# Order of the down units, of the ReLU sums and of a small key copy in a kernel of windowed attention and a low-rank mixer

## Chip, cores and metric

One core of a Trainium2 chip. The metric is the device time of one execution in microseconds (us). The engines have their own in-order queues and meet through semaphores: TensorE (PE, with its weight loads PEld), VectorE (DVE), ScalarE (ACT), GpSimd (POOL) and SyncE (SP, which issues most DMAs here).

## What is computed

Batch 4, 8 heads, 768 positions, head size 64; then a mixer over positions of rank 32 and a two-layer feed-forward of width 2048.

```python
scores = q @ k.T / sqrt(64) - slope[h] * dist      # dist: distance, or 96 for a global key outside the window
keep   = (pos_k < 8) | (0 <= pos_q - pos_k < 96)   # 8 global keys and a window of 96
a      = softmax(where(keep, scores, -1e9));  x = a @ v      # heads side by side: x is 768 x 512 per batch
u      = x + (x.T @ U @ V).T                       # U: 768 x 32, V: 32 x 768
out    = u + relu(u @ w_ch1) @ w_ch2               # 512 -> 2048 -> 512
```

## The kernel before

Attention goes pair of heads by pair of heads: 16 pairs, four to a batch. The pairs 0 to 3 are done in a first stage; from pair 4 on, a loop (L819) takes one step per pair, with i from 4 to 17 ("pair i" below is step i). In it stand the scores of pair i (L366, L373; 128-wide blocks of the diagonal and of the block before it), their scaling and distance term on DVE (L412, L406), the exponentials on ACT (L430), the product with the values of pair i-1 (L443, L447, then reciprocal L452 and scaling L466 on DVE, and a cast to fp16 on POOL, L469), and the mixer of pair i-1: M1 (L478), MT (L495, its result copied from PSUM by DVE at L496, the tile `tmp`), M3 (L532, added into x_sb by DVE at L537 and cast by POOL at L540). Keys and queries of pairs 8 to 15 are loaded in fp32, cast by ACT (L129), turned by DMA transposes that SP issues (L327, L330), and the keys of the neighbour block are put together in `kA` with the eight global keys in front: the rest by ACT (L339), the global columns by DVE (L340).

Between these steps stand slots: `fill(n)` (L731) lets out n units of the feed-forward of an earlier batch. A unit is an "up" (L646: eight 128x256 matmuls into `hps`, then a ReLU on ACT into `htr`, L651) or a "down". Rows are taken in groups of 256, (b, g) with g from 0 to 2. `unit()` (L741) picks: a down may go when the ups of its group are all out and `held[0]` is false; otherwise an up, as long as the ups are not too far ahead; with both possible they alternate.

For batch 0 a down is four 128x512 matmuls (L681): tile t of 128 rows takes four of them (parts 0 to 3, one quarter of w_ch2 each) into one PSUM bank `cps`, opened by the mixer product L675, and DVE adds the bank into x_sb (L686). w_ch2 comes in four pieces, issued by POOL at L230, one for each part.

For the other nine groups (`WG`) the second layer is a Strassen-like product of seven instead of eight (L690, the units x1 y1 x2 y2 x3 y3 x4 on the banks `cx` and `cy`). It needs sums of the ReLU output, s1 = a21 + a22, s2 = s1 - a11, s4 = a12 - s2, s3 = a11 - a21 (in the place of a21), and differences of w_ch2, t1 to t4. `queue_sums` (L621) is called after the fourth and the eighth up of a group and queues each sum in two halves as a job; after a unit, `fill` lets jobs out whose count has been passed (two a unit when more than four are queued, otherwise one). A job is one DVE instruction (L570). `need` (L574) lets out what a product needs and has not got yet. x2 needs s2, y2 s1, x3 s3, y3 s4.

The order of every engine's queue is the order of the program. PSUM has two banks `cps`, three banks `th` (for `hps`, and for the last part of the scores from pair 7 on), one pair `sc` (scores, and M3's result) and one `ob` (values, M1, MT).

Of the kernel before, what the change touches and what calls it, by code (L numbers as in the profile page):

```python
# [16 lines left out]
ALU = mybir.AluOpType  # L17
# [3 lines left out]
def kernel(  # L21
# [13 lines left out]
    nc = tc.nc  # L35
# [3 lines left out]
    P = 128  # L39
# [4 lines left out]
    NJC = DFF // P  # L44
    R = moe_U.shape[1]
    NP = H // 2
# [19 lines left out]
    HJ = NJC // 2  # L66
# [20 lines left out]
    def ps_cps(name):  # L87
        return psum.tile([P, 512], FP32, name=name, tag="cps", bufs=2)
# [29 lines left out]
    def cast_qk(i, *engs):  # L118
        got = []
        for st, nm, eng in zip(staged.pop(i), ("q16", "k16"), engs * 2):  # L120
            st16 = stp.tile([P, NSB, 2, D], FP16, name=nm, tag=nm, bufs=2)
            turn_over = eng.copy if eng is nc.scalar else eng.tensor_copy
            turn_over(st16.rearrange("p n h d -> p h n d"), st)
            got.append(st16)
        cast[i] = got
# [210 lines left out]
    def st_K(i):  # L336
        kT = kts[i]
        kA = kp.tile([P, NSB - 1, P], FP16, name="kA", tag="kA")
        nc.scalar.copy(kA[:, :, NG:], kT.rearrange("d (n p) -> d n p", n=NSB)[:, 0:NSB - 1, NG:])  # L339
        nc.vector.tensor_copy(  # L340
            kA[:, :, 0:NG], kT[:, 0:NG].unsqueeze(1).broadcast_to((P, NSB - 1, NG))
        )
        kas[i] = kA
# [223 lines left out]
    def queue_sum(name, part, out_, a, b_, op, wait=0):  # L567

        def go():
            nc.vector.tensor_tensor(out_, a, b_, op)  # L570
            have.add((name, part))
        (slow if name[0] == "t" else jobs).append((count[0] + wait, go))

    def need(*names):  # L574

        for queue, kind in ((jobs, tuple), (slow, str)):
            while not all(n in have for n in names if isinstance(n[0], kind)):
                queue.popleft()[1]()
# [32 lines left out]
    def queue_group(b, g):  # L611
        ts = slice(g * FT, (g + 1) * FT)
        uT, tmp16, x_sb = uTs[b], tmps[b], xs[b]
        n0, n1 = 2 * g, 2 * g + 1
        cell = {}

        split = (b, g) in WG
        follow = (b, g + 1) if g + 1 < NFG else (b + 1, 0)
        last = (b, g) == (B - 1, NFG - 1)

        def queue_sums(k):  # L621

            h = cell["htr"]
            if k == 0:
                for x in (1, 2, 4):
                    cell[f"s{x}"] = ffp.tile([P, HJ, P], FP16, name=f"s{x}", tag=f"s{x}", bufs=1)
                cell.update(a11=h[:, 0:HJ, 0:P], a12=h[:, HJ:NJC, 0:P],
                            a21=h[:, 0:HJ, P:FT], s3=h[:, 0:HJ, P:FT], a22=h[:, HJ:NJC, P:FT])
            js = slice(k * HJ // 2, (k + 1) * HJ // 2)
            for name, a, b_, op in (  # L630
                ("s1", "a21", "a22", ALU.add), ("s2", "s1", "a11", ALU.subtract),
                ("s4", "a12", "s2", ALU.subtract), ("s3", "a11", "a21", ALU.subtract),
            ):
                queue_sum((name, b, g), k, cell[name][:, js], cell[a][:, js], cell[b_][:, js], op, wait=0 if last else 2)

        def mk_up(at):
            jp = at // 2 + (at % 2) * NJC // 4 if split else at

            def go():
                if jp == 0:  # L640
                    cell["htr"] = ffp.tile([P, NJC, FT], FP16, name="htr", tag="htr", bufs=3)
                hps, done = begun.pop(jp) if jp in begun else (ps_th("hps"), 0)
                for k in range(2):
                    jt = 2 * jp + k
                    for dc in range(done, NDC):
                        nc.tensor.matmul(  # L646
                            hps[:, k * FT:(k + 1) * FT],
                            w1_16[:, dc, jt * P:(jt + 1) * P], uT[:, dc, ts],
                            start=(dc == 0 and k == 0), stop=(dc == NDC - 1 and k == 1),
                        )  # L650
                nc.scalar.activation(  # L651
                    cell["htr"][:, 2 * jp:2 * jp + 2].rearrange("p j t -> p (j t)"), hps, AF.Relu
                )
                if split and at % 4 == 3:
                    queue_sums(at // 4)
            return go

        def store(n, cs=slice(0, DM)):
            def go():
                nc.sync.dma_start(out[b, n * P:(n + 1) * P, cs], x_sb[:, n, cs])  # L660
            if b:
                go()
            else:
                kept.append(go)

        def mk_down(t, part):
            n = 2 * g + t

            def go():
                if (b, g, t, part) == (0, 0, 1, 0):  # L670
                    queue_weight_sums()
                if part == 0:
                    cell["cps"] = ps_cps("cps")
                    if b == 0:
                        nc.tensor.matmul(  # L675
                            cell["cps"], v16w[:, n * P:(n + 1) * P], tmp16,
                            start=True, stop=False,
                        )
                cps, htr = cell["cps"], cell["htr"]
                for jc in range(4 * part, 4 * part + 4):  # L680
                    nc.tensor.matmul(  # L681
                        cps, htr[:, jc, t * P:(t + 1) * P], w2_16[:, jc],
                        start=(b > 0 and jc == 0), stop=(jc == NJC - 1),
                    )
                if part == NJC // 4 - 1:
                    nc.vector.tensor_tensor(x_sb[:, n], cps, x_sb[:, n], ALU.add)  # L686
                    store(n)
            return go

        def mk_product(bank, half, a, w, dst, first=False, done=None):  # L690

            def go():
                if bank not in cell:
                    cell[bank] = ps_cps(bank)
                need(*(((a, b, g), k) for k in range(2) if a[0] == "s"))
                need(*((w, k) for k in range(4 if w == "t3" else 2) if w[0] == "t"))
                ps = cell[bank][:, half]
                for j in range(HJ):
                    nc.tensor.matmul(  # L699
                        ps, cell[a][:, j], weight(w, j), start=(first and j == 0),  # L700
                        stop=(done is not None and j == HJ - 1), skip_group_check=True,
                    )
                n, cs = dst
                nc.vector.tensor_tensor(x_sb[:, n, cs], ps, x_sb[:, n, cs], ALU.add)  # L704
                for what in done or ():
                    store(*what)
            return go

        if b:
            for at in range(NJC // 2):  # L710
                ups_q.append((mk_up(at), (b, g)))
        else:
            first_ups.append([(mk_up(at), (b, g)) for at in range(NJC // 2)])
        if split:
            x1 = mk_product("cx", lo, "a11", "b11", (n0, lo), first=True)
            x2 = mk_product("cx", lo, "s2", "t2", (n0, hi_))
            x3 = mk_product("cx", lo, "s3", "t3", (n1, hi_), done=[(n1, hi_)] if last else None)
            x4 = mk_product("cx", lo, "a22", "t4", (n1, lo), done=[(n1, lo)] if last else [(n1,)])
            y1 = mk_product("cy", lo, "a12", "b21", (n0, lo), first=True)
            y2 = mk_product("cy", hi_, "s1", "t1", (n1, hi_))  # L720
            y3 = mk_product("cy", hi_, "s4", "b22", (n0, hi_), done=[(n0,)])
            for made in (x1, y1, x2, y2, x3, y3, x4):
                downs_q.append((made, (b, g)))
        else:
            for t in range(2):
                for part in range(NJC // 4):
                    downs_q.append((mk_down(t, part), (b, g)))

    ahead, held, kept = [0], [True], deque()

    def fill(n):  # L731
        for _ in range(n):
            unit()
            count[0] += 1
            for _ in range(2 if len(jobs) > 4 else 1):
                for queue in (jobs, slow):
                    if queue and queue[0][0] < count[0]:
                        queue.popleft()[1]()
                        break
# [79 lines left out]
    for i in range(NP, NPAIR + 2):  # L819
# [69 lines left out]
        if live:  # L889
            st_E(i, 0)  # L890
            if i < NPE:
                st_P(i)
        fill(next(units))
        if i >= NPE:
            for _ in range(min(2, len(kept))):
                kept.popleft()()
# [14 lines left out]
            st_X(i - 1)  # L911
        if NPE <= i + 2 < NPE + 2:
            cast_qk(i + 2, nc.gpsimd)
        fill(next(units))
    while ups_q or downs_q:
        fill(1)
# [36 lines left out]
```

## Time and profile before

| what | value |
|---|---|
| three runs | 233.32, 231.82, 234.01 us; median 233.32 |
| profiled execution | 231.37 us; span from first to last instruction 229.6 us |
| granted TensorE clock | 0.998 |
| whole sum of L570 for t, 128x1024 | 0.68 us undisturbed |
| half sum of L570, 128x512 | 0.42 us undisturbed |
| scores' scaling L412 128x1024; L406 128x384 | 1.22 us; 0.55 us |
| eviction L686; adds L704; L537; tmp copy L496 | 0.69; 0.42; 0.96; 0.29 us |
| landing of the w_ch2 pieces after their issue | 7.4 to 14.5 us |

In the profile's rows a group of instructions has its line, engine, operation, tiles (out <- in), shape and count, then busy time in us and the mean of one in ns, then the idle time of the engine in front of them and what ended most of it. In a timeline a row has start, length, engine, line, operation and, in brackets, the idle time before it and its releaser. Matmuls of one run overlap: each starts 0.109 us after the one before at 256 columns (0.216 at 512), while it lasts 0.27 (0.38) to its modelled end.

### The profile page before, as it was taken

To read this page: it belongs to the slowest core of one execution; us is meant where nothing else is said; L and a number is where in the kernel's file an instruction comes from. 1 tells how busy PE (TensorE), PEld (TensorE's weight loads), DVE (VectorE), ACT (ScalarE), POOL (GpSimd) and SP (SyncE) were. 2 spreads that over 40 slices of the span, in tenths; PEclk is the share of its full clock that TensorE was granted. 3 is DMA by queue.
4 is the path that set the end of the run, shared out by engine and by line. 5 is a ranking of instruction groups with operands and counts; after the bars stand their busy time and mean duration, and the time that the engine had idled before them with its cause. 6 is when DMAs were issued, how large, how long until landed. Compare 5 with 4: busy or idle time off the path is not lost.

```text
span 229.6 us, 5883 instructions
## 1 busy us (share of the span) xinstructions
PE 219.3 (96%) x2418; PEld 172.0 (75%) x2420; DVE 158.6 (69%) x346; ACT 125.9 (55%) x196; POOL 70.7 (31%) x115
## 2 busy tenths in 40 slices
PE   7889999999989999998999989999999999999993
PEld 2446678788644546886888868888989888888882
DVE  3688775749586979597979887979764444444452
ACT  6677857685705253958485847392732433333320
POOL 6398637297543423131313131313111000000000
PEclk9999999999999999999999999999999999999999
DMA  6999999989998979999999993751321202010022
GB/s 203 280 291 237 267 221 246 303 159 179 193 170 188 201 184 238 219 232 217 215 245 174 261 178 97 129 174 30 92 67 34 94 0 94 0 69 26 8 86 93
DMA packets 86563, 36.68 MB, mean 160 GB/s; under 512 B 74152, under 2 KB 83592, under 8 KB 86536
## 3 DMA queue, kind: packets, MB, share of 16 engines
q1 hardware_dynamic: 81480, 32.01, 57.5%
q0 software_dynamic: 5056, 4.29, 12.5%
q8 instruction: 19, 0.31, 0.6%
q14 instruction: 8, 0.07, 0.1%
HBM read 27.46 MB, written 6.29 MB: 147 GB/s over the span
## 4 chain that ended last, share of the span: by engine, by line
PE 67%; DVE 11%; DMA 10%; ACT 5%; POOL 4%; issue 1%; SPq 1%; ACTq 0%
PE hps L646 25%; PE cx L699 13%; PE cy L699 10%; PE cps L681 8%; DMA w<-in_moe_w_ch_dram 6%; DMA vst<-in_v_dram 3%; DVE sp L412 3%; PE sc L366 2%; ACT ep L430 2%; PE ob L447 2%; DVE x_sb L466 1%; PE sc L532 1%; PE tp L254 1%; PE ob L443 1%; DVE x_sb L704 1%
## 5 line engine op out<-in xcount | busy, mean ns | idle before, releaser
L646 PE MATMUL hps<-uT,w 128*128 128x256 f16 x756 | 95.5, 273 | 0.2 <-ACT htr L651 0.2
L651 ACT ACTIVATE htr<-hps 128x512 f16<-128x512 f32 x96 | 56.4, 599 | 60.8 <-PE hps L646 60.6
L646 PEld LDWEIGHTS <-w 128*128 128x128 f16 x756 | 71.0, 98 | 9.6 <-issue 0.3
L412 DVE SCALAR_TENSOR_TENSOR sp<-sc,relcat 128x1024 f32<-128x1024 f32 (+1 forms) x27 | 32.1, 1189 | 8.0 <-ACT ep L430 4.3
L430 ACT ACTIVATE ep<-sp 128x1408 f16<-128x1408 f32 x24 | 33.2, 1383 | 0.0
L699 PEld LDWEIGHTS <-htr 128*128 128x128 f16 x288 | 27.7, 98 | 3.4
L704 DVE TENSOR_TENSOR x_sb<-cx,x_sb 128x256 f32<-128x256 f32 x36 | 15.2, 422 | 19.3 <-PE cx L699 18.6
L469 POOL CAST x<-x_sb 128x384 f16<-128x384 f32 x27 | 14.1, 522 | 46.6 <-DVE x_sb L466 43.6
L681 PE MATMUL cps<-w,htr 128*128 128x512 f16 x96 | 23.6, 379 | 1.1 <-DMA w<-in_moe_w_ch_dram 1.1
L540 POOL CAST x<-x_sb 128x768 f16<-128x768 f32 x12 | 11.0, 914 | 43.2 <-DVE x_sb L537 43.2
L699 PEld LDWEIGHTS <-s 128*128 128x128 f16 x216 | 20.2, 98 | 4.3 <-DVE s L570 2.0
L704 DVE TENSOR_TENSOR x_sb<-cy,x_sb 128x256 f32<-128x256 f32 x27 | 11.4, 422 | 12.5 <-PE cy L699 12.3
L466 DVE TENSOR_TENSOR x_sb<-ob,rcp 128x384 f32<-128x384 f32 x30 | 16.7, 558 | 1.0
L366 PEld LDWEIGHTS <-kT 64*128 64x128 f16 x192 | 8.5, 93 | 11.4 <-issue 10.1
L447 PE MATMUL ob<-v,ep 128*128 128x65 f16 x192 | 16.6, 193 | 0.0
L366 PE MATMUL sc<-qT,kT 64*128 64x128 f16 x192 | 15.7, 220 | 0.3 <-DVE x_sb L537 0.2
L681 PEld LDWEIGHTS <-htr 128*128 128x128 f16 x96 | 8.6, 97 | 9.4 <-issue 1.2
L447 PEld LDWEIGHTS <-ep 128*128 128x128 f16 x192 | 13.9, 98 | 2.3 <-issue 0.5
L443 PE MATMUL ob<-vA,ep 128*128 128x65 f16 x160 | 14.4, 194 | 0.4 <-DVE vA L316 0.2
L537 DVE TENSOR_TENSOR x_sb<-sc,x_sb 128x768 f32<-128x768 f32 x12 | 11.5, 956 | 4.6 <-PE sc L532 4.6
L142 POOL CAST v<-vst 128x768 f16<-128x768 f32 x16 | 13.4, 838 | 3.8 <-DMA vst<-in_v_dram 3.8
L373 PE MATMUL sc<-qT,kA 64*128 64x128 f16 x160 | 13.2, 216 | 0.3
(110 smaller groups left out, 320.1 us busy)
## 6 DMA issues: line engine op xcount, KB each, us to landing
qst<-in_q_dram SPq DMA_DIRECT2D x16, 384.0 KB, 5.4
kst<-in_k_dram SPq DMA_DIRECT2D x16, 384.0 KB, 6.4
vst<-in_v_dram SPq DMA_DIRECT2D x16, 384.0 KB, 4.1
out_dram<-x_sb SPq DMA_DIRECT2D x23, 256.0 KB, 3.3
w<-in_moe_w_ch_dram POOLq DMA_DIRECT2D x8, 512.0 KB, 8.6
vA<-v SPq DMA_DIRECT2D x8, 152.3 KB, 4.1
out_dram<-x_sb SPq DMA_DIRECT2D x2, 128.0 KB
uT<-x SPq DMA_TRANSPOSE x12, 3.1
```

Source lines behind the costliest of these rows:

```text
L366: nc.tensor.matmul(scs[hi][:, o:o + P], kT[r, kb * P:(kb + 1) * P], qT[r, kb * P:(kb + 1) * P], start=(o == 0 and not on_pe), stop=(o + P ...
L412: nc.vector.scalar_tensor_tensor(out=sps[i][:, :, c0:c0 + tot], in0=both[:, :, 0:tot], scalar=qk_scale / slope[2 * (i % NP)], in1=relfs[c0 ...
L430: nc.scalar.activation(eps[i][:, hi], sps[i][:, hi], AF.Exp, scale=slope[2 * (i % NP)])
L443: nc.tensor.matmul(ob[:, qi], ep[:, OF[qi - 1]:OF[qi - 1] + P], vA[:, qi - 1, hi], start=True, stop=False,)
L447: nc.tensor.matmul(ob[:, qi], ep[:, DG[qi]:DG[qi] + P], vt[:, qi, hi], start=(qi == 0), stop=True,)
L466: nc.vector.tensor_tensor(xo, ob[:, :, 0:D], rb, ALU.mult)
L469: nc.gpsimd.tensor_copy(x16, xo)
L646: nc.tensor.matmul(hps[:, k * FT:(k + 1) * FT], w1_16[:, dc, jt * P:(jt + 1) * P], uT[:, dc, ts], start=(dc == 0 and k == 0), stop=(dc == ...
L651: nc.scalar.activation(cell["htr"][:, 2 * jp:2 * jp + 2].rearrange("p j t -> p (j t)"), hps, AF.Relu)
L681: nc.tensor.matmul(cps, htr[:, jc, t * P:(t + 1) * P], w2_16[:, jc], start=(b > 0 and jc == 0), stop=(jc == NJC - 1),)
L699: nc.tensor.matmul(ps, cell[a][:, j], weight(w, j), start=(first and j == 0), stop=(done is not None and j == HJ - 1), skip_group_check=True,)
L704: nc.vector.tensor_tensor(x_sb[:, n, cs], ps, x_sb[:, n, cs], ALU.add)
```

## The change

Five edits. Batch 0's first group does the parts 0, 1 and 2 of both its tiles before part 3 of either; since both tiles are open at once, each has its own bank in `cell[t]`. `held[0]` is set anew ahead of the last slot of a step, so that the downs may begin in the last slot of pair 6 and not only in pair 7. In the groups of `WG` except the last, s3 and s4 are queued whole, once all eight ups are out, and s3 ahead of s4; the entries of the second call wait for one unit in place of two. The slot after the first exponential lets no jobs out (`quiet`), and the next unit lets one more out. The global key columns are copied by GpSimd.

In the order of the engines' queues, every unit from the last slot of pair 6 on stands one place sooner than before; DVE has 16 sums and 8 key copies fewer, and POOL the 8 copies, between the cast of v (L142) and the cast after M3 (L540).

```diff
         kA = kp.tile([P, NSB - 1, P], FP16, name="kA", tag="kA")
         nc.scalar.copy(kA[:, :, NG:], kT.rearrange("d (n p) -> d n p", n=NSB)[:, 0:NSB - 1, NG:])
-        nc.vector.tensor_copy(
+        nc.gpsimd.tensor_copy(
             kA[:, :, 0:NG], kT[:, 0:NG].unsqueeze(1).broadcast_to((P, NSB - 1, NG))
         )
...
-            js = slice(k * HJ // 2, (k + 1) * HJ // 2)
             for name, a, b_, op in (
                 ("s1", "a21", "a22", ALU.add), ("s2", "s1", "a11", ALU.subtract),
-                ("s4", "a12", "s2", ALU.subtract), ("s3", "a11", "a21", ALU.subtract),
+                ("s3", "a11", "a21", ALU.subtract), ("s4", "a12", "s2", ALU.subtract),
             ):
-                queue_sum((name, b, g), k, cell[name][:, js], cell[a][:, js], cell[b_][:, js], op, wait=0 if last else 2)
+                parts = {k: slice(k * HJ // 2, (k + 1) * HJ // 2)}
+                if name in ("s3", "s4") and not last:
+                    parts = {0: slice(0, HJ)} if k else {}
+                for part, js in parts.items():
+                    queue_sum(
+                        (name, b, g), part, cell[name][:, js], cell[a][:, js], cell[b_][:, js],
+                        op, wait=0 if last else 2 - k,
+                    )
...
                 if part == 0:
-                    cell["cps"] = ps_cps("cps")
+                    cell[t] = ps_cps("cps")
                     if b == 0:
                         nc.tensor.matmul(
-                            cell["cps"], v16w[:, n * P:(n + 1) * P], tmp16,
+                            cell[t], v16w[:, n * P:(n + 1) * P], tmp16,
                             start=True, stop=False,
                         )
-                cps, htr = cell["cps"], cell["htr"]
+                cps, htr = cell[t], cell["htr"]
...
-                need(*(((a, b, g), k) for k in range(2) if a[0] == "s"))
+                need(*(((a, b, g), k) for k in range(2 if last or a in ("s1", "s2") else 1)
+                       if a[0] == "s"))
...
-            for t in range(2):
-                for part in range(NJC // 4):
-                    downs_q.append((mk_down(t, part), (b, g)))
+            order = [(t, part) for t in range(2) for part in range(NJC // 4)]
+            if (b, g) == (0, 0):
+                order.sort(key=lambda u: u[1] == NJC // 4 - 1)
+            for u in order:
+                downs_q.append((mk_down(*u), (b, g)))
...
-    def fill(n):
+    owed = [0]
+
+    def fill(n, quiet=False):
         for _ in range(n):
             unit()
             count[0] += 1
-            for _ in range(2 if len(jobs) > 4 else 1):
+            pops = owed[0] + (2 if len(jobs) > 4 else 1)
+            owed[0] = 1 if quiet else 0
+            for _ in range(0 if quiet else pops):
                 for queue in (jobs, slow):
...
-        fill(next(units))
+        fill(next(units), quiet=i > NP)
         if i >= NPE:
...
+        held[0] = i < NP + 2
         fill(next(units))
```

## Prediction

> **What bounds the kernel now.** I read the page's busy times first, then busy time by stage, then TensorE's own waits, then the timelines around each of these waits, and last the queue that brings the weights.
>
> ```profile
> PE 219.3 (96%) x2418; PEld 172.0 (75%) x2420; DVE 158.6 (69%) x346; ACT 125.9 (55%) x196; POOL 70.7 (31%) x115
> ...
> 0.00:32.00 32.00, 28.91 (x344) 17.16 (x347) 22.57 (x62) 23.03 (x40) 22.21 (x44) 1.00 1.02 252
> 32.00:60.00 28.00, 27.59 (x344) 22.93 (x343) 17.92 (x29) 21.56 (x34) 17.00 (x26) 1.00 1.09 219
> 60.00:90.00 30.00, 28.71 (x265) 14.81 (x263) 24.69 (x46) 11.77 (x15) 10.91 (x15) 1.00 1.00 200
> 90.00:160.00 70.00, 68.27 (x840) 58.31 (x839) 59.57 (x126) 45.43 (x68) 17.65 (x26) 1.00 0.82 181
> 160.00:180.00 20.00, 19.88 (x215) 17.84 (x213) 12.14 (x31) 8.88 (x15) 2.92 (x4) 1.00 0.28 82
> 180.00:229.60 49.60, 45.93 (x421) 40.92 (x419) 21.66 (x56) 15.20 (x26) 0.00 (x0) 0.99 0.12 44
> ```
>
> The columns of the second view are stretch, length, then busy time of PE, PEld, DVE, ACT and POOL, PE's granted clock, DMA share. PE is idle for 10.3 us of 229.6. Of this 3.1 lie before 32 us, where nothing changes, and 3.7 after its last matmul (the last add and the stores), which stays. The change moves no matmul away; it can only take PE's waits between 60 and 180 us. DVE is the next busiest there (24.7 of 30, then 59.6 of 70), and GpSimd has most of its time free.
>
> ```profile
> PE cx L699 <- DVE s L570: 1.5, 2, 1.0
> PE cps L681 <- DMA w<-in_moe_w_ch_dram: 1.1, 1, 1.1
> PE sc L366 <- DVE x_sb L537: 0.2, 1, 0.2
> PE hps L646 <- ACT htr L651: 0.2, 1, 0.2
> ...
> 59.30 1.04 PE L646 MATMUL hps<-uT,w 128*128 128x256 f16 x8
> 60.51 0.23 PE L366 MATMUL sc<-qT,kT 64*128 64x128 f16 x2 [0.17 <-DVE x_sb L537]
> ...
> 64.91 0.19 PE L447 MATMUL ob<-v,ep 128*128 128x65 f16 x1
> 66.21 1.02 PE L681 MATMUL cps<-w,htr 128*128 128x512 f16 x4 [1.12 <-DMA w<-in_moe_w_ch_dram]
> ...
> 103.13 0.60 PE L699 MATMUL cx<-t,s 128*128 128x256 f16 x4
> 104.22 0.61 PE L699 MATMUL cx<-t,s 128*128 128x256 f16 x4 [0.49 <-DVE s L570]
> ...
> 136.01 0.60 PE L699 MATMUL cx<-t,s 128*128 128x256 f16 x4
> 137.56 0.61 PE L699 MATMUL cx<-t,s 128*128 128x256 f16 x4 [0.96 <-DVE s L570]
> ```
>
> The reader is to see that a shown wait is too short: matmuls are issued one 0.109 us after the other (a unit of eight takes 0.87), while one lasts 0.273 to its modelled end. So I count from when the next start was due. At 60.51: 59.30 + 8 x 0.109 = 60.17 was due, 0.34 lost, of which 0.10 is what each change from hps to sc costs; 0.24. At 66.21: due 64.94, 1.27. At 104.22: due 103.57, 0.65. At 137.56: due 136.45, 1.11. In the same way the PE rows give 0.32 at 100.36 (due 100.03 after the value product), 0.28 at 105.88 and 0.28 at 172.16 (the mixer products of L532, which wait for the tmp copy L496 that stands behind sums on DVE). Together **4.15 us**; that is all that this change can win.
>
> **Part 1: downs a place sooner, third quarter first.** In the orders of the two kernels, one unit stands earlier from here to the end: the last slot of pair 6, empty so far, gets the first down (L675 0.226 + four of 0.216 = 1.09 us), between the mixer products and the scores of pair 7. The 0.24 goes, as the bank is free by then. The fourth w2 piece, issued at 51.7, lands at 66.2. PE's new order walked from 60.17: first part to 61.26, scores to 61.69, second part 62.55, values 62.89, third part 63.75, scores 64.34, t1's first part 65.43, values 65.77, t1's two others 67.50, and only now t0's last part. 67.5 is 1.3 after the landing: the 1.27 goes. The third piece must be in by 62.89, and it lands at 62.7:
>
> ```profile
> w<-in_moe_w_ch_dram POOLq DMA_DIRECT2D x1, 512.0 KB, 11.8
> ```
>
> (issue at 50.96). That is close: bounds 0 and, were it as late as the fourth piece, 66.2 - 62.9 = 3.3; I take 0, as its own row says. Both cps banks are now open until t0's last part is evicted (L686, 0.69), behind one piece of the weight sums and a score pass on DVE: by my walk done at 69.3, and the next tile wants a bank at 69.4. Between 0 and one eviction, 0.7; I take 0.1. Scores of pair 8 come at 72.6 instead of 73.3; qT's transpose is issued at 69.59, held by SP's queue (full until 66.5) and not by PE, and with kT's 2.5 us to landing it is there at 72.1. No wait, 0.5 to spare. Stores of the first tile go late anyway (the kept list), behind transposes on SP that land 3 us before they are used; 0.
>
> **Part 2: the sums let out elsewhere, s3 and s4 whole.** Eight groups trade four halves for two whole sums. Rows on DVE:
>
> ```profile
> L570 DVE TENSOR_TENSOR htr<-htr 128x512 f16<-128x512 f16 x18 | 8.3, 462 | 0.0
> L570 DVE TENSOR_TENSOR s<-htr,s 128x512 f16<-128x512 f16 x18 | 7.7, 429 | 1.2 <-PE cy L699 0.9
> L570 DVE TENSOR_TENSOR t<-w,t 128x1024 f16<-128x1024 f16 x4 | 3.1, 786 | 0.0
> L340 DVE COPY kA<-kT 128x40 f16<-128x40 f16 x8 | 1.3, 167 | 0.2 <-DMA kT<-k 0.2
> ```
>
> A whole sum of this form has no row; the weight sums of the same size take 0.68 undisturbed (median) and 0.79 in the mean, against two halves 0.83 apart and 0.75 back to back (second start 0.33 after the first). Saved per pair -0.04 to +0.15, I take 0.1 (nearest: the same operation in the same size): 1.6 us off DVE's 158.6, none of it by itself on PE's path. What matters is where s2's second half stands. In the new order its entry waits one unit, not two, and s4 and s3 no longer stand ahead.
> Walk of pair 10 (the loop's step i = 10) from the start of its scores (scores 0.66 with both changes, units 0.87, values 0.34; DVE: L412 1.14, reciprocal and scaling 0.7, L406 pair 0.95, L704 0.35 to 0.4): s2 is done at 5.0, and x2 wants it at 6.7. So the 0.65 goes. Whole s3 and s4 end at 8.45, one x2 add follows, tmp is out at 9.05; the mixer products want it at 9.1. The 0.28 goes, hardly. At pair 13 the new order is scores, up, values, x1, scores, y1, values, x2: s2 is done at 5.4, wanted at 5.0; **0.4** of the 1.11 stays. At pair 16 a y2 product now stands between tmp and the mixer product, so the 0.28 there goes. The 0.32 at 100.36 (ACT's k cast waits for its load, the relu stands behind it) goes where it was, since the up before the scores is now relu'd ahead of the cast; at pair 12 the new order repeats the old pattern: between 0 and 0.32, I take 0.2.
> What the new entries delay: the mul of L466 and tmp of L496 are queued behind whole sums, and behind them GpSimd's cast, M1 and the mixer products on PE. Up to 1.4 us (two whole sums) each time; by the walk this is inside two to three units of PE's own work.
>
> **Part 3: key columns on GpSimd.** Eight copies of 0.167 (1.3 us) leave DVE; on GpSimd the nearest row is L295's 128x32 copy, 0.21: 1.7 us on a 31% busy engine. They stand behind the v cast, ahead of the x cast, which waits for DVE anyway (43 us in all). A late kT now holds GpSimd, not DVE (0.24 at 70.8): 0. But the two disturb each other:
>
> ```profile
> 95.25 0.83 POOL L540 CAST x<-x_sb 128x768 f16<-128x768 f32 x1 [3.63 <-DVE x_sb L537]
> 95.42 0.94 DVE L570 TENSOR_TENSOR s<-htr 128x512 f16<-128x512 f16 x1 [0.23 <-ACT htr L651]
> ```
>
> The sum took 0.94 beside a cast that began first, 0.42 alone, so 0.52 is one collision. I take one in front of a wait of PE: 0.5 (bounds 0 and 0.52 at each of the three remaining tight places, 1.6).
> The Trainium skill, "SBUF — State Buffer", section "SBUF: two separate sides", says that GpSimd and a two-input DVE operation share a port pair that one holds for its whole instruction while the other stands still. The row agrees (0.94 against 0.42). By that rule the move to GpSimd can cost DVE 8 x 0.21 = 1.7, more than the 1.3 it gives up; with all of it on PE's path the sum below would be 1.7 worse, 232.2. The rows put most of DVE's sums away from it.
>
> **Sum.** Won 4.15; staying or new 0.1 (bank) + 0.4 (x2, pair 13) + 0.2 (relu) + 0.1 (tmp) + 0.5 (collision) = 1.3. Net 2.85. The profiled execution took 231.37 (its span 229.6 and 1.8 around it): 228.5. The three runs shown have the median 233.32, 1.95 above it (231.82 to 234.01). On the median: **230.5 us**.
>
> **Rivals.**
> *Only part 1 pays.* DVE stays about 85% busy to 160 us, and its waits come back at x2 and L532 in other pairs: won 0.24 + 1.27, 231.8. For it: three tight places of 0.4 us or less in my walk. Against: 3 us less on DVE.
> *The loads set the pace.* DMA is 1.00 busy from 60 to 90 us, and ACT waits 12.7 us in six places for k. If w2's third piece is as late as PE now comes early (0.2 to spare), or k's loads do not come sooner, the 2.85 is given back but for some tenths: 233.0. Against: PE never waited for an input load after 60 us.
> *Slower: whole sums in front of the tmp copy and the next score pass.* s3 and s4 run as one block of 1.4 us; in five groups beside attention it stands ahead of L496 or L412. Each us that PE waits there costs five. It eats the gain from 0.57 per group, and makes the kernel over 1% slower from (2.85 + 2.33) / 5 = 1.04; with the whole 1.4 in each it gives 233.3 - 2.85 + 7.0 = 237.5. Against: by the walk tmp is out in time.
>
> **How the numbers follow.** Forecast 0.54, own range 229.2 (all of the 4.15) to 231.4; only part 1 0.20; loads 0.16; whole sums 0.10. About 1% is what a measurement of this kernel can tell from no change: 231.0 and 235.7 are the bounds. Faster: 0.47 of the forecast and 0.03 of the first rival, 0.50. Slower: the last rival, 0.10. Same: 0.40. The range from 229.1 to 233.4 leaves out the last rival and what noise puts beyond.
>
> **What would show it.** Right: no PE wait on w at about 66 us; x2's waits on s from 1.5 down to some 0.4, at pair 13; no mixer product waiting for tmp; PE's last matmul some 3 us earlier; DVE with 24 fewer instructions. Wrong: a new PE wait on w at 63, on DVE's L692 (the eviction) at 69, or L537 and L412 late behind 128x1024 sums, or GpSimd casts stretched beyond 0.5 and 0.83.

## The result, and the profile after

The change makes the kernel 0.8% faster: the ratio to before is 0.992 (95% interval 0.9901 to 0.9939), with medians of 228.98 us against 231.11 us, 22 runs each. The medians are of all runs; the ratios here and below leave out runs in a slower state, two of them (232.07 and 235.93) among the 22 of after. The first three runs of before (median 233.32) lay high; with 22 runs the median comes to 231.11, beside the profiled 231.37. The profiled execution of after took 229.56 us, its span 227.8 us.

The busy times and the stages of after (columns as before: stretch, length, PE, PEld, DVE, ACT, POOL, granted clock, DMA share, then GB/s):

```profile
PE 218.7 (96%) x2420; PEld 172.0 (76%) x2420; DVE 156.4 (69%) x322; ACT 125.9 (55%) x196; POOL 72.5 (32%) x123
...
60.00:90.00 30.00, 28.83 (x265) 14.74 (x263) 24.82 (x45) 11.56 (x14) 11.95 (x17) 1.00 1.05 201
90.00:160.00 70.00, 69.53 (x855) 59.79 (x855) 58.25 (x113) 45.95 (x71) 18.54 (x32) 1.00 0.82 181
160.00:180.00 20.00, 20.00 (x213) 18.09 (x211) 11.08 (x26) 9.38 (x15) 2.68 (x4) 1.00 0.37 82
```

From 90 to 160 us PE is idle for 0.5 us in place of 1.7. From 60 to 90 it is idle almost as long as before (1.2 against 1.3), though both waits that stood there are gone. The waits of TensorE and the places where they end say why:

```profile
PE hps L652 <- DMA uT<-x: 0.8, 1, 0.8
...
PE cps L687 <- DMA w<-in_moe_w_ch_dram: 0.5, 1, 0.5
...
PE cx L706 <- DVE s L570: 0.3, 1, 0.3
...
63.35 1.02 PE L687 MATMUL cps<-w,htr 128*128 128x512 f16 x4 [0.53 <-DMA w<-in_moe_w_ch_dram]
...
88.87 0.49 PE L652 MATMUL hps<-uT,w 128*128 128x256 f16 x3
90.12 2.12 PE L652 MATMUL hps<-uT,w 128*128 128x256 f16 x18 [0.75 <-DMA uT<-x]
...
133.87 0.60 PE L706 MATMUL cx<-t,s 128*128 128x256 f16 x4
134.74 0.61 PE L706 MATMUL cx<-t,s 128*128 128x256 f16 x4 [0.28 <-DVE s L570]
```

Counted as in the prediction (from when the next start was due), 0.69 us is lost at 63.35 to w2's third piece, 0.92 at 90.12, 0.44 at 134.74 where x2 wants the second half of s2, and 0.20 at 135.7, again at a unit that reads a new uT. With two score passes of 0.09 each this is 2.4 us, against 4.15 before: 1.7 us won. The spans differ by 1.8.

The wait at 90.12 is new. `uT<-x` is the mixed x of batch 1, turned by a DMA transpose that SP issues (L521, `st_X`), four to a batch; the first up of a batch needs the fourth of them in its fourth matmul. With each unit a place sooner, PE now arrives before it. The rows of SP are issues. The first two rows are of before (the transpose and batch 1's first up), the last two of after:

```profile
86.54 1.28 SPq L521 DMA_TRANSPOSE uT<-x  x1
89.92 1.91 PE L646 MATMUL hps<-uT,w 128*128 128x256 f16 x16
...
84.57 1.89 SPq L666 DMA_DIRECT2D out_dram<-x_sb  x2
86.58 1.30 SPq L521 DMA_TRANSPOSE uT<-x  x1
```

The transpose is issued when it was, behind two stores. Before came to its fourth matmul at 90.25 (89.92 + 3 x 0.109) and did not wait; after comes to it at 89.20.

The sums and the key copy, in the groups of after:

```profile
L570 DVE TENSOR_TENSOR htr<-htr 128x1024 f16<-128x1024 f16 x8 | 6.5, 807 | 0.0
L570 DVE TENSOR_TENSOR s<-htr,s 128x1024 f16<-128x1024 f16 x8 | 5.4, 680 | 0.0
L340 POOL COPY kA<-kT 128x40 f16<-128x40 f16 x8 | 2.4, 296 | 3.8 <-DMA kT<-k 3.8
```

A whole s4 takes the 0.68 us that the weight sums showed, a whole s3 0.81 in the mean. That mean is six of 0.68 to 0.69 and two of 1.18 and 1.19, at the pairs 12 and 15, where s3 starts just after a cast on GpSimd. Pair 12, GpSimd, DVE and PE:

```profile
118.01 0.83 POOL L540 CAST x<-x_sb 128x768 f16<-128x768 f32 x1 [2.71 <-DVE x_sb L537]
118.19 1.18 DVE L570 TENSOR_TENSOR htr<-htr 128x1024 f16<-128x1024 f16 x1
...
119.90 1.21 DVE L412 SCALAR_TENSOR_TENSOR sp<-sc,relcat 128x1024 f32<-128x1024 f32 x1
...
121.16 0.23 PE L366 MATMUL sc<-qT,kT 64*128 64x128 f16 x2
```

The score pass ends at 121.11, and the next scores begin at 121.16: the next scores reuse the bank that the pass reads, and these two places are the two score passes of 0.09. The key copy takes 0.30 on GpSimd in place of 0.17 on DVE, and GpSimd waits 3.8 us in front of these copies for kT's transpose.

### The profile page after: what moved, and what is told of

It is laid out like the page before. It is cut to its first block, busy times and chain, and to the rows that moved or that the text cites. A ratio compares the mean times of both kernels' runs of the same rounds, so it can differ in the third digit from the quotient of the medians.

```text
span 227.8 us, 5876 instructions
## 1 busy us (share of the span) xinstructions
PE 218.7 (96%) x2420; PEld 172.0 (76%) x2420; DVE 156.4 (69%) x322; ACT 125.9 (55%) x196; POOL 72.5 (32%) x123
## 3 DMA queue, kind: packets, MB, share of 16 engines
q0 software_dynamic: 5056, 4.29, 12.6%
## 4 chain that ended last, share of the span: by engine, by line
PE 72%; DMA 11%; DVE 9%; POOL 3%; ACT 2%; issue 1%; SPq 0%; DVEq 0%; POOLq 0%
PE hps L652 29%; PE cx L706 13%; PE cy L706 10%; PE cps L687 7%; DMA w<-in_moe_w_ch_dram 6%; DMA kst<-in_k_dram 4%; DVE sp L412 2%; PE sc L366 2%; PE tp L254 2%; PE ob L447 2%; DMA uT<-x 2%; PE sc L532 1%; PE ob L443 1%; PE sc L373 1%; ACT ep L430 1%
## 5 line engine op out<-in xcount | busy, mean ns | idle before, releaser
L412 DVE SCALAR_TENSOR_TENSOR sp<-sc,relcat 128x1024 f32<-128x1024 f32 (+1 forms) x27 | 32.1, 1188 | 8.4 <-PE sc L373 3.9
L706 PEld LDWEIGHTS <-htr 128*128 128x128 f16 x288 | 27.2, 98 | 3.1
L540 POOL CAST x<-x_sb 128x768 f16<-128x768 f32 x12 | 10.5, 874 | 34.8 <-DVE x_sb L537 34.8
L687 PEld LDWEIGHTS <-htr 128*128 128x128 f16 x96 | 8.5, 97 | 8.8 <-issue 0.6
L142 POOL CAST v<-vst 128x768 f16<-128x768 f32 x16 | 13.5, 842 | 3.3 <-DMA vst<-in_v_dram 3.3
L537 DVE TENSOR_TENSOR x_sb<-sc,x_sb 128x768 f32<-128x768 f32 x12 | 11.5, 957 | 4.0 <-PE sc L532 3.9
```

The costliest lines, as they stand in the source:

```text
L412: nc.vector.scalar_tensor_tensor(out=sps[i][:, :, c0:c0 + tot], in0=both[:, :, 0:tot], scalar=qk_scale / slope[2 * (i % NP)], in1=relfs[c0 ...
L687: nc.tensor.matmul(cps, htr[:, jc, t * P:(t + 1) * P], w2_16[:, jc], start=(b > 0 and jc == 0), stop=(jc == NJC - 1),)
L706: nc.tensor.matmul(ps, cell[a][:, j], weight(w, j), start=(first and j == 0), stop=(done is not None and j == HJ - 1), skip_group_check=True,)
```

## Experiments

All ratios are to the kernel before; the diffs are to the kernel after, cut at `...`. The theory at first was a ledger: the time moves by what PE loses in waits, and each part of the change has its own entries. The rivals are in the expectations.

**e1: part 1 alone** (the parts 0 to 2 of both tiles ahead of part 3, called third quarter first, and each unit one place sooner).

```diff
-                if name in ("s3", "s4") and not last:
-                    parts = {0: slice(0, HJ)} if k else {}
...
-                        op, wait=0 if last else 2 - k,
+                        op, wait=0 if last else 2,
...
-        fill(next(units), quiet=i > NP)
+        fill(next(units), quiet=False)
...
-        nc.gpsimd.tensor_copy(
+        nc.vector.tensor_copy(
```

> Only part 1 is done: third quarter first and the downs one place sooner; the sums (halves, s4 before s3, wait 2) and the key columns are as before. Ledger theory (the time moves by PE's waits, and part 1 wins 0.24 + 1.27 us but loses 0.69 to w2's third piece and 0.92 to batch 1's last uT transpose): part 1 by itself is worth -0.1 us; the shifted order also moves the x2 waits (0.65 at pair 11 goes, the one of 1.11 grows to some 1.5 at pair 13), the 0.32 and the 0.28s partly go; in all 0 to -1.0 us, ratio 0.996 to 1.000 of before. Rival (part 1 carries the gain, as the wait on the weights was the longest single one): the whole of the -0.8%, ratio 0.992.

Measured 1.0115 (1.0066 to 1.0164): slower by 1.2%. Neither theory nor rival had that. (Its expectation names pair 11 for the 0.65; it is pair 10.) The timeline of its pair 13, DVE and PE:

```profile
134.03 0.60 PE L703 MATMUL cx<-t,s 128*128 128x256 f16 x4
134.23 0.42 DVE L570 TENSOR_TENSOR s<-htr 128x512 f16<-128x512 f16 x1
134.56 0.19 DVE L452 RECIPROCAL rcp<-ob 128x6 f32<-128x6 f32 x1
134.79 0.56 DVE L466 TENSOR_TENSOR x_sb<-ob,rcp 128x384 f32<-128x384 f32 x1
135.26 1.22 DVE L412 SCALAR_TENSOR_TENSOR sp<-sc,relcat 128x1024 f32<-128x1024 f32 x1
136.40 0.58 DVE L570 TENSOR_TENSOR s<-s,htr 128x512 f16<-128x512 f16 x1
137.03 0.70 PE L703 MATMUL cx<-t,s 128*128 128x256 f16 x4 [2.40 <-DVE s L570]
137.53 1.91 PE L650 MATMUL hps<-uT,w 128*128 128x256 f16 x8
```

One place sooner, x2 comes right after the second values; with the old entries s2's second half is let out only when x2 calls for it, and by then a reciprocal, a scaling and a 1.22 us score pass stand before it on DVE. PE loses 2.57 us there (1.11 before) and 1.19 at x2 of pair 10. The ledger had the direction of the first wait (to 1.5), not its size, and had the second as gone. The last line is worse still: the eight matmuls after the gap take 1.91 us, not 1.03 (see the last section). Counted in the same way, e1 loses some 6.7 us after 57 us, against 4.15 before: these two waits, 1.6 to the slower matmuls, 0.61 at the mixer product at 70.5 us, the rest in small ones. The two transfers for which the expectation had charged it 0.69 and 0.92 were in time.

**e2: the sums and the key columns alone**, in the old order of units.

```diff
-            order = [(t, part) for t in range(2) for part in range(NJC // 4)]
-            if (b, g) == (0, 0):
-                order.sort(key=lambda u: u[1] == NJC // 4 - 1)
-            for u in order:
-                downs_q.append((mk_down(*u), (b, g)))
+            for t in range(2):
+                for part in range(NJC // 4):
+                    downs_q.append((mk_down(t, part), (b, g)))
...
-        held[0] = i < NP + 2
```

> Only the sums and the key columns are changed; order of the downs as before. Ledger theory: the 0.24 and the 1.27 stay, neither transfer is waited for anew, the x2 waits (0.65 and 1.11) and most of the small ones (0.32, 0.28, 0.28) go: -1.7 to -2.3 us, ratio 0.990 to 0.993, as much as the whole change. Rival (part 1 carries the gain): -0.3 us or less, ratio 0.999 to 1.000.

Measured 1.0042 (1.0005 to 1.0079), slower if anything. The ledger's 0.990 to 0.993 is refuted. Its timeline, DVE and PE about the scores of pair 12:

```profile
116.47 0.42 DVE L570 TENSOR_TENSOR s<-htr 128x512 f16<-128x512 f16 x1
...
116.93 0.42 DVE L570 TENSOR_TENSOR s<-s,htr 128x512 f16<-128x512 f16 x1
...
117.28 0.95 DVE L537 TENSOR_TENSOR x_sb<-sc,x_sb 128x768 f32<-128x768 f32 x1
118.14 0.68 DVE L570 TENSOR_TENSOR htr<-htr 128x1024 f16<-128x1024 f16 x1
118.28 0.23 PE L366 MATMUL sc<-qT,kT 64*128 64x128 f16 x2 [0.28 <-DVE x_sb L537]
...
119.08 0.98 DVE L570 TENSOR_TENSOR s<-htr,s 128x1024 f16<-128x1024 f16 x1
119.97 1.21 DVE L412 SCALAR_TENSOR_TENSOR sp<-sc,relcat 128x1024 f32<-128x1024 f32 x1
...
121.24 0.23 PE L366 MATMUL sc<-qT,kT 64*128 64x128 f16 x2 [0.33 <-DVE sp L412]
```

This is in part the mechanism of the prediction's last rival: halves of s1 and s2 stand ahead of L537, and whole s3 and s4 ahead of the score pass L412, so the bank of the scores comes free late. PE loses 0.34 + 0.39 at pair 12, the same again at pair 15 and 0.16 at pair 13; 0.98 stays at x2 of pair 13 and 0.47 at a mixer product. With 0.24 at 60.6 and 0.73 at w2 that makes 4.0 us, about the 4.15 of before: what failed was the forecast of the waits, not the way of counting them.

So the parts are not additive: 1.0115 (of its 1.15%, 0.7% is the slower matmuls of the profiled execution) and 1.0042 alone, 0.992 together. The new theory: the one place sooner is a shift of phase between units and sums. The old sums fit the old phase, the new ones the new phase.

**e3: the key columns back on DVE**, else the change (L340 as in before).

> The change with the global key columns back on DVE. Ledger theory: none of PE's remaining waits is behind these copies but x2's at pair 13; within 0.3 us of the change, ratio to before 0.991 to 0.994. Rival (DVE's load is what pays, 1.3 us of copies less): 0.6 to 1.3 us of the gain goes, ratio 0.995 to 0.998. By the port rule of the Trainium skill (SBUF, section on the two separate sides) it could even be a little faster, since GpSimd's eight copies no longer hold the shared ports.

Measured 0.9927 (0.9898 to 0.9957): the change itself, within its interval. Where the copies stand makes no difference that can be measured, with an interval of 0.3%, or 0.7 us, to either side.

**e4: halves of s3 and s4**, with the new entries and the quiet slot.

```diff
-                if name in ("s3", "s4") and not last:
-                    parts = {0: slice(0, HJ)} if k else {}
...
```

> The change with s3 and s4 in halves again (s3 before s4, entries and quiet slot as in the change). Ledger theory: x3 and y3 come two to five units later than their sums, so whole or half matters little; but the first call now queues four jobs, which stand before the second call's s1 and s2: x2's wait at pair 13 stays at 0.4 or grows to 1: ratio 0.992 to 0.996. Rival (fewer DVE instructions is what pays): 16 instructions more, 1.6 us on DVE, ratio 0.997 to 1.000.

Measured 0.9956 (0.9923 to 0.999): the expected band, but the interval overlaps that of the change. x2's wait at pair 13 is 0.44, as in the change, so the growth that I had thought possible did not come; PE's largest losses there are at the two uTs, 1.38 and 1.05. Whether whole sums by themselves are worth anything stays open.

**e5 to e7: the two new waits on transfers.** e5 takes the parts in pairs, so that w2's third piece is asked for two downs later; e6 puts the two held-back stores of step 8 behind uT's transpose on SP; e7 is both.

```diff
-                order.sort(key=lambda u: u[1] == NJC // 4 - 1)
+                order.sort(key=lambda u: max(1, u[1]))
...
-        if i >= NPE:
+        if i > NPE:
             for _ in range(min(2, len(kept))):
                 kept.popleft()()
...
             st_X(i - 1)
+        if i == NPE:
+            for _ in range(min(2, len(kept))):
+                kept.popleft()()
```

> The change, with batch 0's first group in another order: the parts 0 and 1 of both tiles, then part 2 of both, then part 3 of both. PE then asks for w2's third piece two downs (1.95 us) later. Ledger theory: the 0.69 us at 63 us goes, the fourth piece is still in time, nothing else moves: 0.5 to 0.7 us faster than the change, unless PE, earlier by so much, waits longer for the uT transpose (0.92 now, up to 1.6): then nothing is won by this alone. Rival (the two waits are noise of one execution): no difference.

> The change, with the two held-back stores of the loop's step 8 behind the transpose of uT on SP instead of ahead of it. The stores' issue took 1.9 us just before it (84.57 to 86.46); x16 was cast at 84.75. Ledger theory: uT is issued at 84.8 instead of 86.58 and lands 1.8 us sooner; the 0.92 us at 90.1 goes: 0.7 to 0.9 us faster than the change. Rival (the transpose is held by DMA traffic, not by its place in SP's queue): it lands when it did, no difference.

> The edits of the two runs before together. Ledger theory: both new waits go, 1.4 to 1.6 us faster than the change, ratio to before 0.985 to 0.987. Rival (what PE gains is given back at the next transfer or on DVE): under half of it, ratio 0.989 or more.

Measured 0.9951 (0.9924 to 0.9978), 0.9911 (0.9878 to 0.9945) and 0.9916 (0.988 to 0.9952): none is faster than the change beyond the intervals. In e5 the third piece is not waited for, and the uT at 89.4 then costs 1.24 in place of 0.92, as the expectation allowed; 0.39 is new at a mixer product. In e6 the first uT is issued at 84.36 in place of 86.58 and its wait is gone; the timeline of e6 shows where it went:

```profile
133.84 0.49 PE L652 MATMUL hps<-uT,w 128*128 128x256 f16 x3
135.84 0.70 PE L652 MATMUL hps<-uT,w 128*128 128x256 f16 x5 [1.51 <-DMA uT<-x]
...
127.18 0.85 SPq L111 DMA_DIRECT2D kst<-in_k_dram  x1
128.13 2.01 SPq L666 DMA_DIRECT2D out_dram<-x_sb  x2
130.23 1.37 SPq L521 DMA_TRANSPOSE uT<-x  x1
```

The uT of the next batch stands on SP behind two stores of 2.0 us, and PE, which comes to this unit 1.35 us earlier than in the change (133.84 against 135.19), loses 1.68 us to it (0.20 in the change). In e7 it is 0.94. The rival of e7 was right in the result: the gain was given back at the next transfer.

**e8 to e11, on one chip.** e8 is the change again. e9 is e7 with the two stores of step 12, too, behind the transpose: from M1 of that step on, `store` puts them on a list that is let out after `st_X`. e10 is the change without the place sooner, e11 the change without the third quarter first.

```diff
+        if i == NP + 8:
+            behind[0] = []
         if i > NP:
             st_M1(i - 1)
...
+        if behind[0] is not None:
+            late, behind[0] = behind[0], None
+            for go in late:
+                go()
```

> The change itself once more, on the same chip as the next three, to compare with directly: ratio 0.990 to 0.994 of before. Its waits for uT at 90 and 135 us should vary from run to run with the landing, while their sum with the wait for w2's third piece stays near 1.8 us.

> As e7 (third piece asked for later, uT ahead of the two stores in step 8), and in step 12 the two stores of the second feed-forward group also go behind the transpose of uT, whose issue they held for 2.0 us in e7. Theory now (what is won at w2 and at the first uT is given back at the second uT, 0.94 us at 134.6 in e7, because SP issues its transpose behind the stores): that wait goes too, 0.6 to 0.9 us faster than e7, ratio to before 0.985 to 0.988. Rival (the gain is given back wherever the next transfer or DVE stands, so not by this queue): no faster than e7, ratio 0.990 or more.

> The change without the place sooner: the last slot of step 6 stays empty; third quarter first, new sums and key columns stay. Theory now (the two parts pay only together: one place sooner moves x2, the score passes and the mixer products against the sums): as e2 without its 0.73 at w2, so 0.7 us faster than e2, ratio 0.998 to 1.003, with the score passes again waiting behind whole sums at 118 and 153 us. Rival (what made e2 slow was the order within batch 0): ratio 0.991 to 0.993, as the change.

> The change without the third quarter first: tile 0 does its four parts, then tile 1, one place sooner. PE asks for the fourth piece at about 64.8 (landing 66.2 to 66.7): 0.7 at the third piece and 1.4 to 1.9 at the fourth. Theory: of that, the 0.92 at 90 us (uT) is then no longer waited for, so 0.5 to 1.0 us slower than the change, ratio 0.994 to 0.997. Rival (the order of the parts is worth its whole 1.3 to 1.9 us): ratio 0.998 to 1.000.

Measured: e8 0.993 (0.9899 to 0.9961), the change confirmed. Its third piece came in time; it lost 0.42 at the first uT and 0.72 at the second, 1.1 in all and not the 1.8 that I had expected.

e9 0.9877 (0.9836 to 0.9919), in the expected band. No uT is waited for any more, and SP's issues in step 12 show the swap:

```profile
126.94 0.71 SPq L111 DMA_DIRECT2D kst<-in_k_dram  x1
128.82 1.34 SPq L521 DMA_TRANSPOSE uT<-x  x1
130.26 0.99 SPq L666 DMA_DIRECT2D out_dram<-x_sb  x2
```

The order moves more than the issue. Ahead of the stores the second uT lands 3.3 us (e9) and 3.5 us (e12) after its issue; behind them PE went on only 4.5 (e7) to 5.6 us (e6) after the issue. Whether the stores' own traffic holds the transpose was not tested apart.

e10 0.998 (0.9952 to 1.0008), as expected: the order of batch 0's parts does not rescue the old phase. The score passes wait again (0.34, 0.40, 0.16, 0.34, 0.40 us), x2 loses 0.98. This and e2 show the phase, not batch 0, as what the new sums need. Which of the new entries (one unit's wait, the quiet slot, s3 ahead of s4) needs it was not tested apart.

e11 0.996 (0.9927 to 0.9993), as expected: the fourth piece costs 1.02 at 64.8, and the uT at 90 is then waited for no longer, so only part of it shows. The third piece, for which 0.7 was expected, came in time; 0.40 is lost at a mixer product.

**e12: stores behind the transposes, nothing else.** e9 without its order of parts.

> The change with only the stores put behind the transposes of uT in steps 8 and 12; batch 0's first group keeps the change's order of parts. Theory: both waits for uT go (0.92 + 0.20 in the change's profile, 0.42 + 0.72 in its second); the third piece costs 0 to 0.7 as it happens to land, against 0.40 that the other order of parts paid at the mixer product at 70.8 us: within 0.4 us of e9, ratio 0.986 to 0.990. Rival (the order of parts was the better half of e9): ratio 0.991 or more.

Measured 0.9885 (0.9852 to 0.9918), median 227.96 us against 230.73 of before. PE's waits that are left (all but the one on s at L708 lie before 33 us):

```profile
PE warm L169 <- DVE zw L164: 1.2, 1, 1.2
PE tp L254 <- DVE uT L514: 0.3, 1, 0.3
PE tp L254 <- DVE k L123: 0.3, 1, 0.3
PE cx L708 <- DVE s L570: 0.2, 1, 0.2
PE ob L443 <- DVE vA L316: 0.2, 1, 0.2
```

e9 and e12 beat both kernels by their medians (228.14 and 227.96 us, six runs each); their intervals still overlap that of the change (0.9901 to 0.9939), so the time alone does not settle it, while the waits on uT are gone from both profiles. The order in pairs adds nothing measurable to it.

## Why the prediction was right, and where not

The direction and the bound were right: the gain is PE's waits between 60 and 180 us, 1.7 us of the 1.8 by which the spans differ. The size was 1.2% forecast, 0.8% measured, less than the 1% that I had named as what can be told from no change; to that outcome I gave 0.40. The median of after, 228.98, lies 0.1 us under the range's lower end because I carried a surplus of 1.95 us from three runs over to the forecast. On the base of the forecast the outcome is 0.992 x 233.32 = 231.5, inside the range and 1.0 above the 230.5; against the profiled execution I had forecast 228.5, and it took 229.56, 1.1 above.

*Part 1.* The 0.24 and the 1.27 went as walked. "The third piece must be in by 62.89 ... I take 0": in the profile it landed at 63.3 (50.74 + 12.6) and cost 0.69, in e8 and e12 nothing. This landing took 11.2 us (e8) to 12.6 us (after), so a margin of 0.2 us was none. The rival "The loads set the pace" had named this piece, with nearly the whole 2.85 given back; here it cost 0.69. The wait that failed the sum is one the prediction does not name: batch 1's uT, 0.92 at 90 us. I had looked at every load as late or in time for the place it had, and had checked qT for a PE that comes sooner, but not uT, the other product of SP's queue. The kept stores I had put at 0, "behind transposes on SP that land 3 us before they are used"; here two of them stand ahead of a transpose that PE, a unit sooner, waits for. e9 and e12, where they stand behind it, have no such wait. The 0.1 for the bank did not come.

*Part 2.* x2 at pair 13: 0.4 forecast to stay, 0.44 measured. The waits at x2 of the earlier group, at the relu and at the two mixer products are gone, as walked. In after's rows whole s3 and s4 end at 104.81 and tmp at 105.34, in time for M3. The relu wait of 0.2 and the tmp wait of 0.1 did not come. The collision for which I took 0.5 came twice, 0.50 us each on DVE (s3 beside the cast L540, at the pairs 12 and 15), but only 0.09 of each reached PE.
"Saved per pair ... 0.1": DVE's busy time fell by 2.1 us, of it 1.3 for the key copies, so about 0.05 a pair.

*Part 3.* The move was priced at 0, and e3 agrees as far as its interval tells (0.9927 against 0.992). The two collisions are with the cast L540, which both kernels have, not with the key copies. The key copy's own price was too low (0.21 for 0.30). The Trainium skill, "SBUF — State Buffer", section "SBUF: two separate sides", says that GpSimd and a two-input DVE operation share a port pair that one of them holds for its whole instruction. The prediction took from it a possible loss of 1.7 us of DVE; e3's time shows neither that loss nor a gain.

*What was right by accident.* I added up the parts, 1.5 for part 1 and 2.6 for part 2. Alone they cost 1.2% and 0.4%. The walks were done in the new order with the new sums, so their sum was off by 1.1 us only; their split into parts did not hold at all. That the forecast of the whole came out so near is in part luck: too little was charged for the transfers (0 for 1.81) and too much for the waits on other engines (1.3 for 0.62). The rival "whole sums in front of the tmp copy and the next score pass" holds for the kernel with the old phase (e2, e10); of this one only the 0.18 is left.

The sum again, by profiles: 4.15 won; 0.69 + 0.92 + 0.44 + 0.20 + 0.18 lost; 1.7 net, where I had 1.3 for the lost side.

## To carry to other kernels

In a kernel whose bound engine hardly rests, price an edit by walking the bound engine's queue in its new order against each other queue, transfers included: all that reads something turned, cast or loaded for the next stage is asked for sooner too. What is won early is given back at the next transfer until that queue (here SP: transposes behind stores) is put in order as well. Test the parts alone before crediting them: an order and a schedule of fills tuned to it can each be a loss alone.

## What was not expected of the hardware

In e1 one idle gap of 2.4 us on TensorE was followed by half the granted clock for about 3.4 us. Its stages (columns as above, the granted clock third from the end):

```profile
130.00:134.00 4.00, 4.00 (x67) 3.33 (x62) 3.80 (x8) 2.54 (x4) 0.58 (x2) 1.00 1.18 289
134.00:137.00 3.00, 0.63 (x11) 0.32 (x7) 2.94 (x6) 0.00 (x0) 1.29 (x2) 1.00 1.19 105
137.00:138.00 1.00, 0.97 (x7) 0.75 (x8) 0.23 (x1) 0.00 (x0) 0.00 (x0) 0.71 1.17 269
138.00:139.00 1.00, 1.00 (x6) 0.69 (x5) 0.86 (x3) 0.00 (x0) 0.00 (x0) 0.50 0.83 214
139.00:140.00 1.00, 1.00 (x7) 0.71 (x5) 0.00 (x0) 0.53 (x1) 0.00 (x0) 0.50 0.07 12
140.00:141.00 1.00, 1.00 (x11) 0.72 (x10) 0.00 (x0) 0.07 (x1) 0.00 (x0) 0.58 0.00 0
141.00:142.00 1.00, 1.00 (x17) 0.91 (x15) 0.42 (x1) 0.71 (x2) 0.00 (x0) 1.00 0.00 0
```

Matmuls of 256 columns were 0.213 us apart in place of 0.109, 16 of them, so the gap cost some 1.6 us beyond itself. The profiled execution of e3 has another such gap, 2.72 us up to 26.1 us, and a granted clock of 0.50 from 26 to 32 us. The shorter gaps, up to the 1.51 us of e6, left the clock at 1.00. The slower clock is not the whole of e1's loss: one of its runs had a mean clock of 1.000 and took 232.90 us, longer than every one of the 29 runs of before beside it (at most 232.69). The Trainium skill, "TensorE: Matmul & The Clock Gate", section "Part 1: The HAM clock gate (the "warmup" mystery)", has the half rate set in after an idle window of about 3.4 us; the half rate agrees with the 0.50 here, but the gap before it was 2.4 us, and for this kernel the measured gap counts.
